# Packed attention with a gated MLP: a softmax's exponentials held in written order, and one batch's first scores moved to other PSUM banks

## The chip, the cores and the metric

The kernel runs as one program on one core of a Trainium2 chip. TensorE (PE) does the matrix products, ScalarE (ACT) the exponentials, the Mish activation and casts, VectorE (DVE) maxima, sums, subtractions and 32x32 transposes; SyncE (SP) and GpSimd (POOL) mostly issue DMAs. The metric is device time in microseconds (us), the median of repeated executions. One more execution is recorded by the profiler, and all rows below are of that one.

## The reference

What is computed, in float32, with 8 batches of 8 heads, 576 positions and head width 64, 32 packing queries, model width 512 and a hidden width of 2048:

```python
def sm_attn(qq, kk, vv):
    s = scale * np.matmul(qq, kk.transpose(0, 1, 3, 2))
    s = s - np.max(s, axis=-1, keepdims=True)
    a = np.exp(s)
    a = a / (np.sum(a, axis=-1, keepdims=True) + 1e-09)
    return np.matmul(a, vv)
p_packed = sm_attn(p, k, v)             # first softmax: 32 queries against 576 keys
out = sm_attn(q, p_packed, p_packed)    # second softmax: 576 queries against 32 keys
x = out.transpose(0, 2, 1, 3).reshape(B * S, H * D)
h = x @ w_in
g = h * np.tanh(np.log1p(np.exp(np.minimum(h, 20.0))))   # Mish (h itself past 20)
return g @ w_out
```

## The kernel before, in words

**The loop.** After an opening (some 30 us, written out by hand on all engines) one Python loop runs over t = 16 b + f: batch b = 0 to 7, and in each the 16 groups f of 128 hidden columns. A group does an up-projection (`up(0)` and `up(1)`, lines 790 to 802: six matmuls each, into the two fixed PSUM banks `up_ps[0]` and `up_ps[1]`, over 256 and 320 of the batch's 576 columns), its Mish on ScalarE (`mish`, lines 819 to 826; the second half in two pieces, 256 columns of line 822 and the remaining 64 of line 824), a split of the result into a high and a low part on VectorE (`halves`, lines 828 to 834), and, two groups later, the down-projection into four accumulators (`down`, four chunks of three matmuls, lines 836 to 840). Values are split into high and low parts so that three fast matmuls stand for one in float32. Since one bank belongs to each half, `up(0)` of a group can't start before the Mish of `up(0)` of the group before has read that bank, and so for `up(1)`.

**The attention of the next batch** is threaded through the groups of this one. For batches 2 to 7 (`TOGETHER = 2`) `plan()` (line 622) gives a table of half-steps: `step(2 f)` is called after `up(0)` of group f, `step(2 f + 1)` after the second chunk of `down`. In them stand the transposes of keys and queries (`keys`, `queries`: VectorE, line 452), the first softmax (`score`, `spread`, `exps`), and the second softmax of each half g of the heads: `peak` (maximum and subtraction, lines 299 and 300), `rise` (the exponential on ScalarE, line 306), `share` (sum, reciprocal, product, lines 311 to 320), `back` (transposed back, line 338), `upper` and `lower` (high and low part, lines 341 and 344). `SOFTEN = (17, 25)` puts `peak` of the two halves at half-steps 17 and 25, so `rise` stands at 18 and 26: in the first half of groups 9 and 13, behind `up(0)` and its Mish. Three pieces on TensorE are taken out of the table: at f = 2, 8 and 12 (`SCORE_0, MATCH_0, MATCH_1`) the loop makes an `excursion` (line 911). It computes the scores or the matching products into the first columns of `up_ps[0]` and `up_ps[1]` (`beside=True`) and at once, in the two `ps_a` banks, a quarter of the next product of packed values and `w_in` (`packed_w`, line 750). In such a group (`away`) `up(0)` comes late, after the third chunk of `down`.

**What sets the order.** TensorE's instructions run as they are written (`manual_schedule`). From batch 1 on, those of the other engines are put in order by a planner at build time, which goes by a simulated time. `tc.keep_in_program_order(x)` holds one instruction behind the one that was written before it on its engine; it adds an order, no wait. Before the change this is done for `queries`, for the splitting of `w_out` (line 120) and for some transposes of batch 2 (`pinned`).

**Which table.** ScalarE evaluates the exponential and Mish from different function tables, and an `ACT_TABLE_LOAD` stands ahead of each first use. In the trace such a load has the line of the instruction that needs it: 306 or 495 for an exponential, 822 for the Mish that follows.

Of the kernel before, what the change touches and what calls it, by code (L numbers as in the profile page):

```python
# [12 lines left out]
AF = mybir.ActivationFunctionType  # L13
# [13 lines left out]
SCORE_0, MATCH_0, MATCH_1 = 2, 8, 12  # L27
# [6 lines left out]
TOGETHER = 2  # L34
# [9 lines left out]
def body(  # L44
# [10 lines left out]
    nc = tc.nc  # L55

    B, H, S, D = q.shape
# [15 lines left out]
    scale = 1.0 / float(D) ** 0.5  # L73
# [101 lines left out]
    class Batch:  # L175
# [127 lines left out]

        def rise(self, gs):
            a2 = self.a2[:, gs].rearrange("a h g n -> a (h g) n")
            nc.scalar.activation(out=a2, in_=a2, func=AF.Exp, scale=scale)

        def tally(self, gs):
            a2 = self.a2[:, gs].rearrange("a h g n -> a (h g) n")
# [67 lines left out]
    class Later(Batch):  # L377
# [244 lines left out]
        def plan(self):  # L622

            self.by = None
            self.kT, self.qT = {}, {}
            first = 0 if self.b == TOGETHER else 2
            steps = {
                first: [self.start, lambda: self.keys(0)],
                first + 1: [lambda: self.keys(1)],
                4: [lambda: self.queries(0)],  # L630
                7: [lambda: self.score(1)],
                8: [lambda: self.queries(1)],
                9: [self.exps],
                11: [lambda: [None for _ in self.turn_weights()]],
                12: [lambda: self.sums(self.exped)],
                15: [lambda: self.turned(0), lambda: self.turned(1)],
            }
            for g, n in enumerate(SOFTEN):
                gs = slice(g, g + 1)
                steps[n] = [lambda gs=gs: self.peak(gs)]  # L640
                steps[n + 1] = [lambda gs=gs: self.rise(gs)]
                steps[n + 2] = [lambda gs=gs: self.share(gs)]
                steps[n + 3] = [lambda g=g: self.back(g), lambda g=g: self.upper(g)]
                steps[n + 4] = [lambda g=g: self.lower(g)]
            return steps
# [206 lines left out]
    def down(grp, c):  # L852
        b, f = grp.b, grp.f
        if f == 0 and c == 0:
            accs[:] = [ps_acc.tile([P, DO], F32, name=f"acc{i}", tag="acc") for i in range(NCH)]
        cs = slice(c * P, (c + 1) * P)
        if b == 0:
            nc.tensor.matmul(out=accs[c], lhsT=grp.act[:, cs], rhs=wo[f], start=f == 0, stop=f == NF - 1)  # L858
        else:
            down_one(accs[c], grp.g[0], grp.g[1], cs, f, f == 0, f == NF - 1)  # L860
        if f < NF - 1:
            return
        final = b == B - 1 and c >= NCH - 2
        o = evac(accs[c], c + final)
        queue = (nc.scalar, nc.sync if b == B - 1 else nc.gpsimd)[(c + final) % 2]
        for dst, lo, hi in batches[b].rows(c):
            queue.dma_start(out=dst, in_=o[lo:hi, :])  # L867
# [113 lines left out]
    with tc.manual_schedule(engines={mybir.EngineType.PE}):  # L981
# [54 lines left out]
        steps = {}  # L1036
        g_rest = None
        for t in range(n_groups + LAG):
            b, f = divmod(t, NF)
            grp = None  # L1040
            if t < n_groups:
# [5 lines left out]
                if f == 0 and TOGETHER <= b + 1 < B:  # L1047
                    steps = batches[b + 1].plan()
# [9 lines left out]
                if t == 1:  # L1058
                    grp = ahead
                else:  # L1060
                    grp = Group(b, f, None if t == 2 else wps[b, f // 4 if b else f // 2], g_rest)
# [28 lines left out]
                join(3)  # L1090
            if dn:
                down(dn, 0)
            away = grp and TOGETHER <= b + 1 < B and f in (SCORE_0, MATCH_0, MATCH_1)
            if away:
                flush()
                excursion(b, f)
# [103 lines left out]
```

## Time and profile before

| what | us |
|---|---|
| median of 3 runs | 742.53 (742.35 to 742.55) |
| the profiled execution, its own time | 743.13 |
| its span, from the first to the last instruction | 741.3 |
| around the span | 1.8 |
| TensorE matmuls busy | 722.1 (97%) |
| VectorE busy | 430.0 (58%) |
| ScalarE busy | 314.5 (42%) |
| GpSimd busy | 71.1 (10%) |

How to read it: TensorE runs nearly all the time, at a granted clock of 0.999 of full speed. A matmul's end is modelled, and matmuls overlap: three of 512 columns start 0.23 us apart although each is listed with some 0.40 us. Idle time of TensorE is therefore best read from the starts. A timeline row has the start, the duration, the engine, the line, the operation and, in square brackets, how long the engine was idle before it and what ended that.

### The profile page before, as it was taken

The page shows a single profiled execution, that of the slowest core. Times are in us where ns is not written, and L with a number is a line of the kernel's source. Part 1 is how long each engine was busy: PE and PEld are TensorE (multiplying, and loading weights), DVE is VectorE, ACT ScalarE, POOL GpSimd, SP SyncE. Part 2 cuts the span into 40 slices and gives each one's busy share as a digit, 9 for nine tenths or more (in the row PEclk, how much of TensorE's full clock was granted, in tenths as well). Part 3 has the DMA queues.
Part 4 walks back from the last instruction along what each step waited for, and adds up shares of the span by engine and source line. Part 5 has one row for each costly group of instructions (what it writes and reads, how often), then busy time and mean ns, then how long its engine had stood idle before and what let it go on. Part 6 is the DMA issues. An engine that isn't in the chain of part 4 may idle for free.

```text
span 741.3 us, 12735 instructions
## 1 busy us (share of the span) xinstructions
PE 722.1 (97%) x5094; PEld 554.3 (75%) x5094; DVE 430.0 (58%) x763; ACT 314.5 (42%) x710; POOL 71.1 (10%) x103
## 2 busy tenths in 40 slices
PE   8899999999999999999999999999999999999997
PEld 5455656687787787887888877877878777888885
DVE  4999887847747466547545576373663655442332
ACT  4777655535534244344332444243442433332221
POOL 0585540000000000000000000000000000000000
PEclk9999999999999999999999999999999999999999
DMA  9999962552203612144012442034101000010002
GB/s 235 307 285 243 283 119 56 102 82 58 33 25 75 109 32 33 62 68 97 13 19 78 66 97 33 37 69 81 33 1 44 29 1 1 1 57 1 1 0 72
DMA packets 187114, 56.34 MB, mean 76 GB/s; under 512 B 175024, under 2 KB 177328, under 8 KB 187056
## 3 DMA queue, kind: packets, MB, share of 16 engines
q1 hardware_dynamic: 183376, 47.14, 28.7%
q10 hardware_dynamic: 2336, 4.20, 1.5%
q0 software_dynamic: 1344, 4.20, 1.5%
q8 instruction: 40, 0.66, 0.4%
q14 instruction: 18, 0.15, 0.1%
HBM read 46.07 MB, written 9.44 MB: 75 GB/s over the span
## 4 chain that ended last, share of the span: by engine, by line
PE 76%; DVE 11%; ACT 6%; DMA 2%; SPq 2%; issue 2%; DVEq 0%; POOL 0%; ACTq 0%
PE ps_h L800 23%; PE acc L838 12%; PE acc L840 12%; PE acc L839 12%; PE acc L858 5%; PE ps_w L714 2%; ACT L822 2%; DVE xT L452 2%; PE ps_rest L840 2%; PE ps_rest L839 2%; PE ps_rest L838 2%; DVE a L300 1%; DMA q_t<-in_q_dram 1%; PE ps_h L467 1%; DVE mx L299 1%
## 5 line engine op out<-in xcount | busy, mean ns | idle before, releaser
L822 ACT ACTIVATE g<-ps_h 128x256 f32<-128x256 f32 (+2 forms) x256 | 96.4, 385 | 264.6 <-PE ps_h L800 236.1
L838 PE MATMUL acc<-wo_hi,g_hi 128*128 128x512 f32 x448 | 179.3, 400 | 0.0
L840 PE MATMUL acc<-wo_hi,g_lo 128*128 128x512 f32 x448 | 177.1, 395 | 0.0
L839 PE MATMUL acc<-wo_lo,g_hi 128*128 128x512 f32 x448 | 176.7, 394 | 0.0
L800 PE MATMUL ps_h<-aT_hi,wp_hi 128*128 128x256 f32 x496 | 154.7, 312 | 8.7 <-ACT g L822 5.9
L833 DVE CAST g_hi<-g 128x512 fp32r<-128x512 f32 x112 | 47.5, 424 | 195.2 <-ACT g L822 195.0
L800 PE MATMUL ps_h<-aT_lo,wp_hi 128*128 128x256 f32 x496 | 146.5, 295 | 0.2 <-DVE aT_lo L344 0.2
L800 PE MATMUL ps_h<-aT_hi,wp_lo 128*128 128x256 f32 x496 | 146.3, 295 | 0.0
L800 PEld LDWEIGHTS ps_h<-aT_hi,wp_hi 128*128 128x128 f32 x496 | 93.5, 188 | 29.7 <-ACT g L822 10.7
L838 PEld LDWEIGHTS acc<-wo_hi,g_hi 128*128 128x128 f32 x448 | 84.3, 188 | 31.9 <-issue 16.8
L800 PEld LDWEIGHTS ps_h<-aT_lo,wp_hi 128*128 128x128 f32 x496 | 93.5, 189 | 11.8 <-issue 3.4
L840 PEld LDWEIGHTS acc<-wo_hi,g_lo 128*128 128x128 f32 x448 | 84.1, 188 | 21.4 <-DVE g_lo L834 2.0
L800 PEld LDWEIGHTS ps_h<-aT_hi,wp_lo 128*128 128x128 f32 x496 | 93.5, 189 | 0.0
L839 PEld LDWEIGHTS acc<-wo_lo,g_hi 128*128 128x128 f32 x448 | 84.1, 188 | 9.2
L834 DVE TENSOR_TENSOR g_lo<-g,g_hi 128x512 fp32r<-128x512 f32 x112 | 77.1, 688 | 7.2 <-DVE g_hi L833 0.5
L858 PE MATMUL acc<-wo,g 128*128 128x512 f32 x128 | 61.3, 604 | 0.0
L725 ACT CAST wp_hi<-ps_w 128x512 fp32r<-128x512 f32 x56 | 30.1, 591 | 65.0 <-PE ps_w L714 65.0
L726 DVE TENSOR_TENSOR wp_lo<-ps_w,wp_hi 128x512 fp32r<-128x512 f32 x56 | 35.9, 683 | 8.8 <-ACT wp_hi L725 8.8
L867 POOL DMA_DIRECT2D out_dram<-o x16 | 9.2, 575 | 328.1 <-DVE o L847 324.1
L858 PEld LDWEIGHTS acc<-wo,g 128*128 128x128 f32 x128 | 22.4, 189 | 22.8 <-issue 19.2
L714 PE MATMUL ps_w<-wi,ppT 64*32 64x512 f32 (+1 forms) x576 | 36.9, 548 | 2.2 <-DVE wi L700 1.5
L824 ACT ACTIVATE g_rest<-ps_h 128x64 f32<-128x64 f32 x128 | 28.3, 221 | 0.0
(135 smaller groups left out, 778.5 us busy)
## 6 DMA issues: line engine op xcount, KB each, us to landing
w_st<-in_moe_w_in_dram SPq DMA_DIRECT2D x16, 512.0 KB, 7.8
w_st<-in_moe_w_out_dram SPq DMA_DIRECT2D x16, 512.0 KB, 7.3
q_n<-in_q_dram SPq DMA_DIRECT2D x56, 144.0 KB, 3.1
v_n<-in_v_dram SPq DMA_DIRECT2D x56, 128.0 KB, 2.8
k_n<-in_k_dram SPq DMA_DIRECT2D x32, 144.0 KB, 3.2
out_dram<-o ACTq DMA_DIRECT2D x14, 256.0 KB, 2.1
k_n<-in_k_dram SPq DMA_DIRECT2D x96, 32.0 KB, 2.0
out_dram<-o POOLq DMA_DIRECT2D x12, 256.0 KB, 2.5
```

The source lines that it names most:

```text
L714: nc.tensor.matmul(out=ps[h * NP:(h + 1) * NP, :], lhsT=ppTb[row:row + D, g, h * NP:(h + 1) * NP], rhs=w[row:row + D], start=True, stop=Tr ...
L725: nc.scalar.copy(out=hi, in_=ps)
L726: nc.vector.tensor_tensor(out=lo, in0=ps, in1=hi.bitcast(F32), op=ALU.subtract)
L800: nc.tensor.matmul(out=ps, lhsT=w[:, fs], rhs=a[:, g, cs], start=(n == 0), stop=(n == 5))
L822: nc.scalar.activation(out=self.act[:, a:a + m], in_=ps[:, :m], func=AF.Mish)
L824: nc.scalar.activation(out=self.g_rest[self.b % 2][self.f // 4][:, self.f % 4, :], in_=ps[:, m:n], func=AF.Mish)
L833: nc.vector.tensor_copy(out=hi, in_=self.act)
L834: nc.vector.tensor_tensor(out=lo, in0=self.act, in1=hi.bitcast(F32), op=ALU.subtract)
L838: nc.tensor.matmul(out=acc, lhsT=hi[:, cs], rhs=wh, start=start, stop=False)
L839: nc.tensor.matmul(out=acc, lhsT=hi[:, cs], rhs=wl, start=False, stop=False)
L840: nc.tensor.matmul(out=acc, lhsT=lo[:, cs], rhs=wh, start=False, stop=stop)
L858: nc.tensor.matmul(out=accs[c], lhsT=grp.act[:, cs], rhs=wo[f], start=f == 0, stop=f == NF - 1)
```

## The change

Three things are changed. `rise` returns its instruction, and the table of batches 2 to 7 wraps it in `keep_in_program_order`: each of those twelve exponentials is held behind the ScalarE instruction written before it, the Mish of `up(0)` of group 9 or 13. The excursion at f = 2 is dropped for the first batch that is planned this way (b + 1 = 2, so in batch 1): its `score(0)` stands at half-step 4 instead, behind `up(0)` of group 2, and goes into the two `ps_a` banks, while its quarter of `packed_w` falls to the ordinary place at the end of group 2. And `queries(0)` moves from half-step 4 to 5 in all planned batches.

```diff
         def rise(self, gs):
             a2 = self.a2[:, gs].rearrange("a h g n -> a (h g) n")
-            nc.scalar.activation(out=a2, in_=a2, func=AF.Exp, scale=scale)
+            return nc.scalar.activation(out=a2, in_=a2, func=AF.Exp, scale=scale)
...
                 first + 1: [lambda: self.keys(1)],
-                4: [lambda: self.queries(0)],
+                4: [lambda: self.score(0)] if self.b == TOGETHER else [],
+                5: [lambda: self.queries(0)],
                 7: [lambda: self.score(1)],
...
                 steps[n] = [lambda gs=gs: self.peak(gs)]
-                steps[n + 1] = [lambda gs=gs: self.rise(gs)]
+                steps[n + 1] = [lambda gs=gs: tc.keep_in_program_order(self.rise(gs))]
                 steps[n + 2] = [lambda gs=gs: self.share(gs)]
...
-            away = grp and TOGETHER <= b + 1 < B and f in (SCORE_0, MATCH_0, MATCH_1)
+            away = grp and TOGETHER <= b + 1 < B and f in (SCORE_0, MATCH_0, MATCH_1)[b + 1 == TOGETHER:]
             if away:
                 flush()
                 excursion(b, f)
```

## Rows read from the trace of the kernel before

**Rows 1.** The page's busy time of each engine: us, share of the span, instructions.
```profile
PE 722.1 (97%) x5094; PEld 554.3 (75%) x5094; DVE 430.0 (58%) x763; ACT 314.5 (42%) x710; POOL 71.1 (10%) x103
```
**Rows 2.** Waits, TensorE alone, 127 to 650 us: us in total, times, longest.
```profile
PE ps_h L800 <- ACT g L822: 5.9, 11, 0.6
PE ps_h L800 <- ACT g_rest L824: 1.4, 2, 0.7
PE ps_h L800 <- DVE a L487: 1.4, 2, 1.2
```
**Rows 3.** Timeline of ScalarE, groups 8 and 9 of batch 2.
```profile
260.94 1.28 ACT L306 ACT_TABLE_LOAD   x1
262.49 0.69 ACT L306 ACTIVATE a<-a 128x576 f32<-128x576 f32 x1 [0.27 <-DVE a L300]
263.19 1.28 ACT L822 ACT_TABLE_LOAD   x1
264.49 0.66 ACT L822 ACTIVATE g<-ps_h 128x256 f32<-128x256 f32 x2
...
266.00 0.39 ACT L822 ACTIVATE g<-ps_h 128x256 f32<-128x256 f32 x1 [0.73 <-PE ps_h L800]
...
268.20 0.38 ACT L822 ACTIVATE g<-ps_h 128x256 f32<-128x256 f32 x1 [0.80 <-PE ps_h L800]
268.48 0.22 ACT L824 ACTIVATE g_rest<-ps_h 128x64 f32<-128x64 f32 x1
```
**Rows 4.** Timeline of TensorE, groups 9 and 10 of batch 2.
```profile
263.71 0.40 PE L839 MATMUL acc<-wo_lo,g_hi 128*128 128x512 f32 x1
263.94 0.40 PE L840 MATMUL acc<-wo_hi,g_lo 128*128 128x512 f32 x1
264.93 0.39 PE L800 MATMUL ps_h<-aT_hi,wp_hi 128*128 128x256 f32 x1 [0.59 <-ACT g L822]
...
267.13 0.31 PE L800 MATMUL ps_h<-aT_hi,wp_hi 128*128 128x320 f32 x1
...
268.00 0.40 PE L838 MATMUL acc<-wo_hi,g_hi 128*128 128x512 f32 x1
...
271.50 0.30 PE L800 MATMUL ps_h<-aT_hi,wp_hi 128*128 128x320 f32 x1
```
**Rows 5.** Timeline of TensorE, group 5 of batch 1, behind the first softmax.
```profile
148.37 0.38 PE L800 MATMUL ps_h<-aT_hi,wp_hi 128*128 128x256 f32 x1 [0.35 <-ACT g L822]
```
**Rows 6.** Line 306, 160 to 660 us: count, duration ns min/median/max, first and last start.
```profile
L306 ACT ACT_TABLE_LOAD  x12: 1283/1283/1283, 172.4 to 629.7; - x12
```
**Rows 7.** Timeline of ScalarE, first softmax in batch 2 (`exps`).
```profile
236.47 1.28 ACT L495 ACT_TABLE_LOAD   x1
237.77 1.17 ACT L495 ACTIVATE a<-a 128x1152 f32<-128x1152 f32 x1
...
240.25 0.66 ACT L822 ACTIVATE g<-ps_h 128x256 f32<-128x256 f32 x2
```
**Rows 8.** Timeline of VectorE, second softmax in batch 2, both halves.
```profile
261.70 0.76 DVE L300 TENSOR_TENSOR a<-a,mx 128x576 f32<-128x576 f32 x1
...
267.43 0.76 DVE L344 TENSOR_TENSOR aT_lo<-at,aT_hi 128x576 fp32r<-128x576 f32 x1 [0.21 <-ACT aT_hi L341]
...
287.51 0.76 DVE L344 TENSOR_TENSOR aT_lo<-at,aT_hi 128x576 fp32r<-128x576 f32 x1 [0.21 <-ACT aT_hi L341]
```
**Rows 9.** Timelines of ScalarE and TensorE, group 13 and the start of batch 3.
```profile
286.08 0.39 ACT L822 ACTIVATE g<-ps_h 128x256 f32<-128x256 f32 x1 [0.74 <-PE ps_h L800]
...
298.23 0.28 PE L800 MATMUL ps_h<-aT_hi,wp_hi 128*128 128x256 f32 x1
```
**Rows 10.** Timelines of TensorE and VectorE, group 2 of batch 1, the excursion.
```profile
130.64 0.87 PE L467 MATMUL ps_h<-xT,pT 64*32 64x288 f32 x16
...
135.20 0.39 PE L800 MATMUL ps_h<-aT_hi,wp_hi 128*128 128x256 f32 x1 [1.23 <-DVE a L487]
...
134.63 0.94 DVE L487 TENSOR_SCALAR a<-ps_h,top 128x288 f32<-128x288 f32 x2
```

## The prediction

> **What bounds the kernel now.** I began with the page's busy time: TensorE's matmuls are busy for 722 us of a 741 us span, VectorE for 430 and ScalarE for 315 [rows 1]. So TensorE sets the time, its instructions run in written order, and an edit that neither removes nor adds matmuls can only act on the gaps between them. The second view is therefore the list of waits for TensorE alone, over the stretch in which batches 2 to 7 get their attention. Everything it waited for stands in three rows: 11 waits on the Mish of line 822 (5.9 us), 2 on the small Mish of line 824 (1.4 us), and 2 on VectorE's line 487, of which one has 1.2 of the 1.4 us [rows 2].
>
> The third view is the order of time around one of the Mish waits. In batch 2, ScalarE loads the exponential's table at 260.94, waits 0.27 us for the subtraction of line 300, does the exponential of the second softmax, loads Mish's table back, and only at 264.49 gets to the Mish of group 8, two of them in a row [rows 3]. TensorE had finished its chunk of `down` and wanted `up(0)` of group 9, whose bank that first Mish still had to read. Matmuls of the chunk start 0.23 us apart (263.71, 263.94), so the next was due at 264.17; it came at 264.93 [rows 4]. That is a stall of 0.76 us, listed as 0.59 because a modelled 0.40 us matmul counts as busy for 0.17 us past the next one's due start.
>
> So the exponential, written for group 9 behind the Mish of its `up(0)`, runs ahead of both Mish of group 8. The block of load, exponential and load stands in the way of a Mish that TensorE needs soon.
>
> How many of the 13 Mish waits are of this kind? One is the first softmax's in batch 1 (0.35 us) [rows 5], which the change doesn't touch. The other twelve lie one each beside the twelve exponentials of line 306, whose table loads run from 172.4 to 629.7 us [rows 6]. They hold 5.9 + 1.4 − 0.35 = 6.95 us as listed, and with 0.17 us each for the modelled ends 6.95 + 2.04 = 9.0 us. I use 8.9, as the listed sums are rounded.
>
> **Part 1, the exponentials held back.** Nothing is removed: twelve loads of 1.28 us [rows 6], twelve exponentials and twelve loads back remain. The block moves behind the Mish of `up(0)` of group 9 (13). What is late next? I place it in batch 2 step by step, in the times of the old trace less the 0.76 us that the stall gave. `up(0)` of group 9 starts at 264.17. Its Mish began 1.07 us after such a start (264.93 to 266.00) and takes 0.39 us [rows 3, 4], so it ends at 265.63. Load, exponential and load add 1.28 + 0.69 + 1.28 and some 0.05 between them: 268.93. The exponential is done at 267.63. Its operand was ready at 262.46 [rows 8], so no wait for VectorE returns.
>
> The instruction queued behind the block is the Mish of `up(1)` of group 9. It takes 0.50 us with its small piece (268.20 to 268.70) [rows 3], so the bank is free at 269.43. `up(1)` of group 10 asks for it at 271.50 − 0.76 = 270.74 [rows 4]. **The margin is 1.3 us**, so this wait costs nothing here. In batches 1, 3 and 5, twelve more matmuls of the remaining columns (`down_rest`) stand before that point, and the margin is larger by theirs.
>
> A row of the old trace shows the same shape without cost: the first softmax of batch 2 has a block of 3.8 us (236.47 to 240.25), with two Mish queued behind [rows 7], and the waits list has only one such stall in the whole run, in batch 1 [rows 2, 5].
>
> VectorE's sum, product and transposes follow the exponential. From its end (263.18) to the end of the low part (268.19) it was 5.0 us [rows 3, 8]. The split of group 9's Mish stands behind some of these; it is wanted only by `down` of group 11, over 2 us after the Mish. For the second half, the Mish of group 13 moves from 286.08 to 284.5, the exponential ends at 287.0, and the low part at 292.0. Batch 3's first `up(0)`, the first reader, starts at 298.23 less two stalls, 296.7 [rows 8, 9]. The margin is 4.7 us. So I cost part 1 at nothing and take its whole gain: **8.9 us**, bounds 4.5 (half the stalls turn up again one Mish later) and 9.0.
>
> In this trace a switch of tables costs what its load is listed with: the exponential of line 495 starts 0.02 us after its load ends [rows 7]. The Trainium skill, ScalarE: Activation LUTs (What ACT_TABLE_LOAD costs), speaks against this placement: it gives 1.28 us for the load and about 1.38 us more for a drain, 2.66 us for each switch. By that rule the block would end 2.8 us later and overrun the margin by 1.5 us.
>
> **Part 2, the first scores of batch 2.** In batch 1 the excursion at 130.64 writes its scores into the banks of `up`, and `up(0)` of group 2 waits until VectorE's last subtraction has left them: 1.23 us listed, 1.40 with the modelled end [rows 10]. With the scores in the `ps_a` banks this wait goes. A new one is possible: `packed_w` at the end of group 2 needs both `ps_a` banks. Between the scores and it stand three chunks of `down` (3 × 0.69) and `up(1)` (0.87, from 267.13 to 268.00 [rows 4]), 2.9 us. In the old trace the two subtractions ended at 135.57, 4.1 us after the scores (131.51) [rows 10], with older VectorE work in between. The old lag kept gives a wait of 1.2 us and next to no gain; the spread done within 2.9 us gives the whole 1.4 us. `score(1)` waits in turn for `packed_w`'s results to leave the same banks, with three chunks of `down` and `up(0)` between; no row has this. Its bounds are nothing and 0.7 us, and I take nothing. The scores now start 0.7 us later (behind `up(0)`), when more of the older work is done, so I take the middle: **0.7 us gained**, bounds −0.5 and 1.4.
>
> **Part 3, `queries(0)` half a step later.** Between half-steps 4 and 5 only `down`, `up(0)` and its Mish are written: nothing on VectorE, SP or POOL in batches 2 to 6. It stays behind the same VectorE instruction, and its loads behind the same DMAs. In batch 1 it only follows the moved scores. Cost nothing, bounds −0.2 and 0.2 us, a small share of the stalls in [rows 2].
>
> **The sum.** 8.9 + 0.7 = 9.6 us off the profiled execution's 743.13 gives 733.5. The median of the runs lies 0.6 us lower, at 742.53: 732.9, and I say **733.0**.
>
> **Rivals.**
>
> First, the stall is moved, not removed: the Mish behind the block comes late for `up(1)` of group 10. For it speaks that ScalarE's order is the planner's, which may put a cast ahead; against it the 1.3 us margin and [rows 7]. If half of the twelve stalls return (the six of batches 2, 4 and 6, with no `down_rest`), it gives 733.0 + 4.5 = 737.5. Chance 0.12.
>
> Second, it doesn't do what it says: the hold is only behind one instruction, and if the Mish of group 9 were itself moved, or the block fell ahead of another Mish that is needed at once, all twelve stalls would stay, at about 742. Nothing in the trace speaks for it except that the planner chose the early place. Chance 0.07.
>
> Third, slower: the second half's high and low parts come too late for the next batch's first `up(0)`. That decides once the chain ends more than 4.7 us later than I place it. At two groups later than placed (8.8 us), six borders lose 4.1 us each, 24.6 − 9.6 = 15 us net: 757.5. Against it, the exponential is held behind one instruction that ends at 265.6 and then nothing else is in its way. Chance 0.04.
>
> Fourth, longer switches: two Mish and an exponential so close together might cost more than the listed loads. It decides from 1.3 us on. If each switch took one load time more, 2 × 1.28 − 1.3 = 1.3 us would be lost in the six cases without `down_rest`, 7.6 us: 740.6. The loads take 1.283 us without exception [rows 6], and line 495 starts at once [rows 7]. Chance 0.03. (The Trainium skill's drain, named above, would be such a cost.)
>
> **How the numbers follow.** The forecast has 0.74, with a range of its own from 732 to 735. The range for 8 in 10 reaches from 731.7 (all of both parts, and 0.5 us for the spread of runs) to the first rival at 737.5. About 0.2% (1.5 us) is what a measurement of this kernel can tell from no change. Faster by more than that: the forecast, the first and the fourth rival, 0.89. Within it: the second, 0.07. Slower: the third, 0.04.
>
> **What would show it.** Right: no wait of TensorE on line 822 or 824 beside the twelve blocks; in ScalarE's timeline the block between the two Mish of group 9 and of 13; the same 12 loads of line 306; the Mish after the block over before `up(1)` of the next group by about 1.3 us. In group 2 of batch 1 no wait on line 487 before `up(0)`; what is left stands before line 714. Wrong: waits of `up(1)` on Mish in groups 10 and 14; a wait of a batch's first `up(0)` on line 341 or 344; or exponentials still ahead of group 8's Mish.

## The result, and the profile after

| | before | changed | ratio |
|---|---|---|---|
| median, first measurement | 742.54 us (742.35 to 743.48, 4 runs) | 731.68 us (731.47 to 731.83, 4 runs) | 0.9851 (95%: 0.9834 to 0.9868) |
| median, second measurement | 742.14 us (741.68 to 744.44, 9 runs) | 731.72 us (731.51 to 732.18, 4 runs) | 0.9856 (95%: 0.9842 to 0.9870) |
| profiled execution, its span | 743.13, 741.3 us | 731.83, 730.0 us | |

The change makes the kernel 1.5% faster: 10.9 us by the first measurement, 10.4 by the second. The forecast was 9.6 us off and 733.0, and the first median lies 0.02 us below the low end of the range, 731.7. The direction and the mechanism held; the gain was larger than the sum, and one term of the sum was too small (below). The two measurements differ by 0.4 us, nearly all of it in the medians of the kernel before (742.54 and 742.14).

TensorE still sets the time. The page of the changed kernel, busy time of each engine and then the chain of work that ended last, by engine:

```profile
PE 718.6 (98%) x5094; PEld 554.9 (76%) x5094; DVE 429.6 (59%) x763; ACT 315.3 (43%) x710; POOL 71.1 (10%) x103
...
PE 90%; DVE 4%; DMA 3%; ACT 2%; SPq 1%; issue 1%; POOL 0%; DVEq 0%; ACTq 0%
```

The counts are those of [rows 1], so no work went or came.

The list of waits for TensorE alone, 127 to 650 us, the same view as [rows 2] (lines behind the edit have moved by one: 800 is now 801, 822 is 823):

```profile
PE ps_w L715 <- DVE a L487: 0.4, 1, 0.4
PE ps_h L801 <- ACT g L823: 0.3, 1, 0.3
PE ps_h L801 <- DVE a L487: 0.2, 1, 0.2
```

Of the 13 waits for a Mish one is left, the first softmax's in batch 1, as in [rows 5]. All twelve beside the second softmax are gone. The wait of `up(0)` in group 2 of batch 1 is gone too, and one of 0.4 us ahead of `packed_w` (line 715) has come.

ScalarE in order of time, groups 8 to 10 of batch 2, to be held against [rows 3]:

```profile
260.51 0.39 ACT L823 ACTIVATE g<-ps_h 128x256 f32<-128x256 f32 x1 [1.14 <-DVE wp_lo L727]
260.80 0.22 ACT L825 ACTIVATE g_rest<-ps_h 128x64 f32<-128x64 f32 x1
261.99 0.39 ACT L823 ACTIVATE g<-ps_h 128x256 f32<-128x256 f32 x1 [0.98 <-PE ps_h L801]
262.39 1.28 ACT L306 ACT_TABLE_LOAD   x1
263.69 0.69 ACT L306 ACTIVATE a<-a 128x576 f32<-128x576 f32 x1
264.39 1.28 ACT L823 ACT_TABLE_LOAD   x1
265.69 0.39 ACT L823 ACTIVATE g<-ps_h 128x256 f32<-128x256 f32 x1
265.97 0.22 ACT L825 ACTIVATE g_rest<-ps_h 128x64 f32<-128x64 f32 x1
```

Both Mish of group 8 now come ahead of the block, and so does the first of group 9 (261.99). The one that waits is the second of group 9, whose bank is free at 266.19.

TensorE, groups 9 and 10 of batch 2, to be held against [rows 4]:

```profile
260.78 0.40 PE L841 MATMUL acc<-wo_hi,g_lo 128*128 128x512 f32 x1
261.02 0.28 PE L801 MATMUL ps_h<-aT_hi,wp_hi 128*128 128x256 f32 x1
261.13 0.28 PE L801 MATMUL ps_h<-aT_lo,wp_hi 128*128 128x256 f32 x1
...
265.39 0.28 PE L801 MATMUL ps_h<-aT_hi,wp_hi 128*128 128x256 f32 x1
...
267.49 0.30 PE L801 MATMUL ps_h<-aT_hi,wp_hi 128*128 128x320 f32 x1
```

`up(0)` of group 9 starts 0.24 us after the last matmul of `down`, at once. `up(1)` of group 10 starts at 267.49, 1.3 us after its bank was free: the margin that the prediction read out of the old trace.

### The profile page after: what moved, and what is told of

It reads as the page before. It is cut to its first block, busy times and chain, and to the rows that moved or that the text cites. A ratio compares the mean times of both kernels' runs of the same rounds, so it can differ in the third digit from the quotient of the medians.

```text
span 730.0 us, 12752 instructions
## 1 busy us (share of the span) xinstructions
PE 718.6 (98%) x5094; PEld 554.9 (76%) x5094; DVE 429.6 (59%) x763; ACT 315.3 (43%) x710; POOL 71.1 (10%) x103
## 4 chain that ended last, share of the span: by engine, by line
PE 90%; DVE 4%; DMA 3%; ACT 2%; SPq 1%; issue 1%; POOL 0%; DVEq 0%; ACTq 0%
PE ps_h L801 25%; PE acc L839 15%; PE acc L841 14%; PE acc L840 14%; PE acc L859 5%; PE ps_w L715 4%; PE ps_rest L841 2%; PE ps_rest L840 2%; PE ps_rest L839 2%; PE ps_h L467 2%; DMA q_t<-in_q_dram 1%; PE ps_h L536 1%; DMA q_n<-in_q_dram 1%; PE ps_a L516 1%; PE ps_s L467 1%; PE ps_h L813 1%
## 5 line engine op out<-in xcount | busy, mean ns | idle before, releaser
L311 DVE TENSOR_REDUCE sm<-a 128x18 f32<-128x576 f32 (+1 forms) x15 | 11.9, 792 | 28.3 <-ACT a L306 28.3
```

## Where the extra microsecond was

Three explanations of the surplus were open. **A**: a stall costs more than its wait. **B**: the moved scores gave more than 0.7 us. **C**: the surplus lies in the opening, which was 0.8 us shorter in the changed kernel's profile, be it by the change or by chance.

For A, the trace of before already holds a row that the sum didn't use. The weight loads of TensorE (PEld) in the kernel before, around the stall of [rows 4], and the two matmuls behind it:

```profile
263.71 0.19 PEld L840 LDWEIGHTS acc<-wo_hi,g_lo 128*128 128x128 f32 x1
264.93 0.19 PEld L800 LDWEIGHTS ps_h<-aT_hi,wp_hi 128*128 128x128 f32 x1 [1.03 <-ACT g L822]
...
265.15 0.27 PE L800 MATMUL ps_h<-aT_lo,wp_hi 128*128 128x256 f32 x1
265.26 0.28 PE L800 MATMUL ps_h<-aT_hi,wp_lo 128*128 128x256 f32 x1
```

The first matmul of the stalled `up(0)` starts at 264.93 [rows 4], and so does the load of its weights: it waited together with the matmul. Its successor starts 0.22 us later, where 0.11 or 0.12 us is usual (265.15 to 265.26; in the changed kernel 261.02 to 261.13). In the changed kernel that load is early, 0.23 us ahead of its matmul at 261.02:

```profile
260.79 0.19 PEld L801 LDWEIGHTS ps_h<-aT_hi,wp_hi 128*128 128x128 f32 x1
261.02 0.19 PEld L801 LDWEIGHTS ps_h<-aT_lo,wp_hi 128*128 128x128 f32 x1
```

So a stall costs its wait and about 0.10 us behind it, called the restart from here on. Comparing the starts of the same matmuls in both traces, the distance between the kernels grows by 0.75 us at the first matmul of `up(0)` of group 9 in batch 2 and by another 0.11 us at the second, and so at each of the twelve places, by 0.49 to 0.90 us and then by 0.10 or 0.11 (in batch 1 at `up(1)`). Twelve waits give 8.86 us and twelve restarts 1.23 us: 10.1 us.

That the late weight load is the reason of the restart is read from rows, and other rows of the changed kernel support it. Of its 448 first matmuls of a chunk of `down`, 420 have their load ahead, and the next matmul starts 0.22 to 0.24 us later. The other 28 stand behind small matmuls of another shape; their load starts together with the matmul, and the next one starts 0.34 us later, although none of them waited for another engine:

```profile
136.26 0.19 PEld L839 LDWEIGHTS acc<-wo_hi,g_hi 128*128 128x128 f32 x1 [0.84 <-issue]
...
136.26 0.50 PE L839 MATMUL acc<-wo_hi,g_hi 128*128 128x512 f32 x1
136.60 0.39 PE L840 MATMUL acc<-wo_lo,g_hi 128*128 128x512 f32 x1
```

No run changes the place of the load alone, so the price is measured and its reason is not shown by an edit.

## The experiments

**Only the exponentials held.** The edit is `rise` and its line in the table, as in the change; `score(0)` and `queries(0)` stay.

```diff
-                steps[n + 1] = [lambda gs=gs: self.rise(gs)]
+                steps[n + 1] = [lambda gs=gs: tc.keep_in_program_order(self.rise(gs))]
```

> Only the twelve exponentials of the second softmax are held behind the Mish written before them; the scores of batch 2 and queries(0) stay where they were. Theory A (a stall of TensorE costs the wait and 0.10 us more, because the first matmul after it starts without its weights loaded ahead): 8.87 us of waits and 12 x 0.10 us give 10.1 us, so about 732.4. Theory B (a stall costs only the wait, and the surplus over the forecast came from the moved scores): 8.9 us, about 733.6. Theory C (the surplus lies in the opening, and is no effect of the change): 8.9 to 10.1 us, and the opening as long as before.

Measured: 733.02 us (732.26 to 733.97, 4 runs) against 742.51, ratio 0.9872 (0.9859 to 0.9886): 9.5 us, with runs that lie 1.7 us apart. The median lies between A and B and doesn't decide; the trace is sharper. Its waits of TensorE, 127 to 650 us:

```profile
PE ps_h L800 <- DVE a L487: 1.3, 1, 1.3
PE ps_h L800 <- ACT g L822: 0.3, 1, 0.3
```

All twelve are gone, and the distance to the kernel before grows by 10.1 us (from 0.55 us in batch 0 to 10.64 us behind the last of the twelve), in twelve steps of 0.5 to 0.9 us each followed by one of 0.10 or 0.11. This is A's number.

**Only the scores and `queries(0)` moved**, the exponentials left free (the change without the line above).

> The scores of batch 2 and queries(0) moved as in the change, the exponentials not held. Theory A: the wait of 1.40 us at up(0) goes and a wait before packed_w of 0.4 us listed comes, net 0.4 us: about 742.1, no difference that can be told. Theory B: 1.5 to 2 us, about 740.8.

Measured: 742.05 us (741.68 to 743.26, 11 runs) against 742.51, ratio 0.9995 (0.9987 to 1.0004). Its waits of TensorE, 127 to 650 us:

```profile
PE ps_h L801 <- ACT g L823: 5.9, 11, 0.6
PE ps_h L801 <- ACT g_rest L825: 1.4, 2, 0.7
PE ps_w L715 <- DVE a L487: 0.3, 1, 0.3
```

The Mish waits are those of [rows 2] to the digit; the 1.2 us on line 487 became 0.3 us ahead of `packed_w`. The starts of the same matmuls gain 0.50 us across groups 2 and 3 of batch 1. That is 0.5 us from both measures, though the interval takes in no difference at all. B falls.

**Only `queries(0)` moved.**

```diff
-                4: [lambda: self.queries(0)],
+                5: [lambda: self.queries(0)],
```

> Only queries(0) moved from half-step 4 to 5. Both theories: no difference (742.5, within 0.3 us), and the same order of instructions on VectorE and SP.

Measured: 742.96 us (741.92 to 744.86, 11 runs) against 742.51, ratio 1.0004 (0.9995 to 1.0013): the medians are 0.45 us apart, a little more than expected, but the interval takes in no difference. The order of the instructions is that of the kernel before, on every engine.

**Half of the exponentials held**, those of group 9.

```diff
-                steps[n + 1] = [lambda gs=gs: self.rise(gs)]
+                steps[n + 1] = [lambda gs=gs, g=g: self.rise(gs) if g else tc.keep_in_program_order(self.rise(gs))]
```

> Only the six exponentials of the first half of the heads are held (group 9), those of group 13 stay early. Six waits of 4.32 us together go (0.82 + 3 x 0.75 + 0.75 + 0.49). Theory A: 4.32 + 6 x 0.10 = 4.9 us, about 737.6. Theory B: 4.3 us, about 738.2. In the trace the distance between two starts of up(0) one group apart shows which: 0.85 us shorter in a batch of the middle, or 0.75.

Measured: 737.40 us (737.22 to 737.62, 5 runs) against 742.51, ratio 0.9931 (0.9919 to 0.9943): 5.1 us. From the starts, 4.3 us of waits and 6 × 0.10 us of restarts, 4.9 us. The waits that are left are those of group 13 (the one on `g_rest` is batch 1's), the first softmax's, and the excursion's on line 487:

```profile
PE ps_h L800 <- ACT g L822: 3.2, 6, 0.6
PE ps_h L800 <- DVE a L487: 1.5, 1, 1.5
PE ps_h L800 <- ACT g_rest L824: 0.7, 1, 0.7
```

The six steps are those of the run with all twelve held, each to 0.01 us, and group 13 keeps its stalls: each half accounts for its own, with no exchange between them.

**The margin, tried from the other side.** Behind each of the twelve held exponentials ScalarE gets a copy of zeros that nobody reads.

```diff
+        def longer(self, gs):
+            tc.keep_in_program_order(self.rise(gs))
+            spare = att.tile([P, 6 * P], F32, name="spare", bufs=1)
+            tc.keep_in_program_order(nc.scalar.copy(
+                out=spare.rearrange("p (t x) -> p t x", x=P), in_=still.unsqueeze(1).to_broadcast([P, 6, P])
+            ))
...
-                steps[n + 1] = [lambda gs=gs: tc.keep_in_program_order(self.rise(gs))]
+                steps[n + 1] = [lambda gs=gs: self.longer(gs)]
```

> The changed kernel with a copy of 128x768 zeros put behind each of the twelve exponentials on ScalarE, some 0.8 us more in the block. If the margin before up(1) of group 10 is the 1.3 us read from the trace, this costs nothing: the changed kernel's time within 0.3 us, and up(1) waits for no Mish. If the block costs ScalarE's time in any other way: up to 12 x 0.8 = 10 us.

Measured: 731.97 us (731.81 to 732.36, 4 runs), where the changed kernel beside it had 731.72. Twelve copies of 0.82 us put 9.8 us of ScalarE's time inside the block; the medians differ by 0.25 us, and the runs overlap (731.51 to 732.18 for the changed kernel). TensorE waits for no Mish but the first softmax's (lines have moved by 7 or 8: 808 is the old 800, 830 the old 822):

```profile
PE ps_h L808 <- ACT g L830: 0.3, 1, 0.3
PE ps_w L722 <- DVE a L494: 0.3, 1, 0.3
PE ps_h L808 <- DVE a L494: 0.2, 1, 0.2
```

**The same with a longer one.** The cut is against the run above.

```diff
-            spare = att.tile([P, 6 * P], F32, name="spare", bufs=1)
+            spare = att.tile([P, 18 * P], mybir.dt.uint8, name="spare", bufs=1)
...
-                out=spare.rearrange("p (t x) -> p t x", x=P), in_=still.unsqueeze(1).to_broadcast([P, 6, P])
+                out=spare.rearrange("p (t x) -> p t x", x=P), in_=still.unsqueeze(1).to_broadcast([P, 18, P])
```

> The same with a cast of 128x2304 zeros, some 2.1 us more in the block. The margin of 1.3 us is overrun by 0.8 us where no matmuls of the remaining columns stand before up(1) of group 10 (14): in batches 2, 4 and 6, six times. With 0.10 us for the start without loaded weights: 6 x 0.9 = 5.4 us over the changed kernel, about 737.4. In batches 1, 3 and 5 (margin larger by twelve matmuls, 2.7 us) nothing. If no margin matters: 0; if all twelve: 10.8 us.

Measured: 736.44 us (736.29 to 736.72, 5 runs), 4.7 us over the changed kernel. The first row of TensorE's waits, and then ScalarE and TensorE around the first of the six:

```profile
PE ps_h L808 <- ACT g_rest L832: 3.5, 6, 0.6
```

```profile
263.16 0.69 ACT L306 ACTIVATE a<-a 128x576 f32<-128x576 f32 x1
263.75 2.10 ACT L311 CAST spare<-still 128x2304 uint8<-128x2304 f32 x1
265.87 1.28 ACT L830 ACT_TABLE_LOAD   x1
267.16 0.38 ACT L830 ACTIVATE g<-ps_h 128x256 f32<-128x256 f32 x1
267.44 0.22 ACT L832 ACTIVATE g_rest<-ps_h 128x64 f32<-128x64 f32 x1
```

```profile
266.74 0.39 PE L848 MATMUL acc<-wo_hi,g_lo 128*128 128x512 f32 x1
267.71 0.41 PE L808 MATMUL ps_h<-aT_hi,wp_hi 128*128 128x320 f32 x1 [0.59 <-ACT g_rest L832]
267.97 0.31 PE L808 MATMUL ps_h<-aT_lo,wp_hi 128*128 128x320 f32 x1
```

`up(1)` of group 10 was due at 266.97 and starts at 267.71, 0.74 us late. By the starts each of the six stalls, in batches 2, 4 and 6 alone, costs 0.75 us and 0.11 us behind it, 5.1 us together. Their place and length are those of the prediction's margin of 1.3 us, overrun by some 0.8 (2.10 − 1.3), and the price confirms A with stalls that were made by an edit.

**The changed kernel once more**, for C.

> The changed kernel once more, beside the next three. By theory A (a stall costs its wait and 0.10 us) the edits are worth 10.1 + 0.4 = 10.5 us against the kernel before, about 732.0; the 0.8 us by which the opening was shorter in its first profile should not be there in the median. If the opening is an effect of the change: about 731.3.

Measured: 731.72 us against 742.14, 10.4 us off. A's 10.5 us is met without the opening. In its profile the first split matmul of `up` starts at 50.03 us, in ten profiled executions of this study anywhere from 49.65 to 50.79, and the kernel before had the latest. The same view in the kernel before and in the one with the longer copy:

```profile
50.79 0.68 PE L800 MATMUL ps_h<-aT_hi,wp_hi 128*128 128x256 f32 x1
```

```profile
49.65 0.68 PE L808 MATMUL ps_h<-aT_hi,wp_hi 128*128 128x256 f32 x1
```

Up to 130 us all ten kernels have the same instructions in the same order on every engine, so no edit acts on the opening through the order, and the profile of before was a long execution, by 0.6 us over its median. C isn't needed. It isn't excluded to the last tenth either: the three kernels without any hold have the three latest openings (50.40 to 50.79, against 49.65 to 50.23), which these runs don't explain, and of the first measurement's 10.9 us some 0.4 stay over A's sum.

**One step further**: the first softmax's exponential of batch 2 held too, which was the one Mish wait left.

```diff
-            nc.scalar.activation(out=a, in_=a, func=AF.Exp, scale=scale)
+            x = nc.scalar.activation(out=a, in_=a, func=AF.Exp, scale=scale)
+            if self.b == TOGETHER:
+                tc.keep_in_program_order(x)
```

> The changed kernel with the first softmax's exponential of batch 2 held in written order too, which leaves the wait at up(0) of group 5 in batch 1 (0.35 us listed). By theory A it goes with 0.17 us for the modelled end and 0.10 us: 0.6 us below the changed kernel, about 731.4, if nothing waits behind the moved block. If the block, 3.7 us there, is late for up(1): no gain.

Measured: 731.01 us (730.78 to 731.42, 4 runs), ratio to the kernel before 0.9846 (0.9832 to 0.9860): 0.7 us below the changed kernel, whose runs beside it (731.51 to 732.18) don't overlap with these. It is the fastest version of the study, by 0.1%. The block now stands behind the Mish of group 4's `up(0)` (825 is the old 822):

```profile
143.41 0.39 ACT L825 ACTIVATE g<-ps_h 128x256 f32<-128x256 f32 x1 [0.26 <-PE ps_h L803]
143.81 1.28 ACT L495 ACT_TABLE_LOAD   x1
145.11 1.17 ACT L495 ACTIVATE a<-a 128x1152 f32<-128x1152 f32 x1
146.29 1.28 ACT L825 ACT_TABLE_LOAD   x1
```

By the starts it gains 0.51 + 0.10 us at `up(0)` of group 5. The profile has a single wait in the stretch, `up(0)` of group 2 (0.3 us), whose Mish came late behind a cast that waited for a DMA; no other kernel's profile had it, and these runs don't show what set that DMA back.

## Why the prediction was right, and where it was short

**What bounds.** Right. The twelve waits were beside the twelve exponentials, and all went with the order.

**Part 1, the place of the block.** Right in each step. The Mish followed its `up(0)` by 0.97 us (1.07 forecast), the exponential ended 264.38 − 261.02 = 3.36 us after that start (forecast 267.63 − 264.17 = 3.46), and the margin before `up(1)` was 1.3 us, as forecast. From the exponential's end to the end of the low part it was 4.7 us (5.0). For the second half, the low part ended at 288.22 and batch 3's first `up(0)` started at 293.33:

```profile
287.46 0.76 DVE L344 TENSOR_TENSOR aT_lo<-at,aT_hi 128x576 fp32r<-128x576 f32 x1 [0.21 <-ACT aT_hi L341]
```

```profile
293.33 0.28 PE L801 MATMUL ps_h<-aT_hi,wp_hi 128*128 128x256 f32 x1
```

That is a margin of 5.1 us, where 4.7 was forecast. VectorE now waits longer for the exponential (2.32 us before a sum in batch 2), which costs nothing.

**Part 1, its price.** Here the step failed: "with 0.17 us each for the modelled ends 6.95 + 2.04 = 9.0 us. I use 8.9". The term was a stall's price, taken as the lateness of the first matmul. As lateness it was right (8.86 us by the starts), but a stall's price measures 0.84 us instead of 0.74 on average, since the matmul behind it is late by 0.10 us more: 10.1 us in place of 8.9. The upper bound of 9.0 was wrong by the same step, and so the low end of the range: with 10.1 in its sum it would have been 742.53 − 10.1 − 1.4 − 0.5 = 730.5. Besides, 731.7 goes with 8.9 and not with the bound of 9.0, which gives 731.6. [rows 4] had the sign of it, a first matmul listed with 0.39 us where its like takes 0.28.

**Part 2.** Right in kind, at the upper end in size: 0.7 us forecast, 0.39 us by the starts in the changed kernel's first profile, 0.67 in its second, 0.51 with this part alone. In the first the new wait stood where it was named, ahead of `packed_w`; in the second it is not in the list of waits, so the middle that was taken between two bounds came out by luck in part. VectorE in the first profile of the changed kernel, group 2 of batch 1:

```profile
132.50 0.69 DVE L118 TENSOR_TENSOR wo_lo<-wo,wo_hi 128x512 fp32r<-128x512 f32 x1
133.11 0.82 DVE L483 TENSOR_REDUCE mx<-ps_s 128x1 f32<-128x288 f32 x2
133.96 0.16 DVE L485 TENSOR_TENSOR top<-mx 128x1 f32<-128x1 f32 x1
134.15 0.94 DVE L487 TENSOR_SCALAR a<-ps_s,top 128x288 f32<-128x288 f32 x2
```

The scores were there at 131.23 (130.52 and 0.71), but the spread began only at 133.11, behind older work on VectorE, and left the banks at 135.09. **Part 3** was nothing, as forecast.

**The rivals.** The first, a stall that moves on, did not occur, but the longer copy made it: a copy of 0.82 us makes no stall, one of 2.10 us makes six. Of the second and the third the waits list shows nothing. The fourth, longer switches, falls by the rows above: the exponential of line 306 starts 0.02 us after its load in the changed kernel too (262.39 + 1.28 to 263.69). The Trainium skill's page ScalarE: Activation LUTs (What ACT_TABLE_LOAD costs) counts some 1.38 us of drain on top of a load; no switch in these traces shows it, and with it the 1.3 us margin would not have held.

## What to carry to other kernels

Where one engine runs at 97% in a fixed order, look at the few waits that it has and at what the planner of another engine has put in front of the work it waits for; the same block a half-step later cost nothing here. Before moving a block, work out the margin to the next reader, because it says both that the move is free and how much more it would bear. Take a stall's price from the distance between the same two instructions with and without it, several instructions behind it, and not from the listed idle time.

## What the runs showed of the hardware

A TensorE stall cost 0.10 to 0.11 us beyond its wait, the same at twelve natural and six made stalls. The first weight load stands behind the same wait as its matmul (idle for 1.03 us), where it otherwise runs 0.23 us ahead. At 28 places without a wait where the load also started with its matmul, the next matmul was late by the same 0.10 to 0.11 us (0.34 instead of 0.23). Executions of one kernel were spread over 0.4 to 2.9 us in a set, and the opening alone by 1.1 us across ten profiles, so a single profiled execution may stand off its median by more than a small edit is worth.
